# The first product of groups 3 to 6 of a routed attention and ELU kernel: four of seven block products cut once more into seven small ones

## The chip, the cores and the metric

The kernel runs on one core of a Trainium2 chip. Time is device time in microseconds (us) for one execution. The kernel before takes 914.18 us, the median of 3 runs (912.76 to 914.26). The profile comes from one further execution.

## What is computed

```python
attn = routing_attention(q, k, v, centroids)          # [4, 8, 768, 64], only within equal clusters
x = attn.transpose(0, 2, 1, 3).reshape(3072, 512)
h = x @ w_in                                          # [3072, 512] @ [512, 2048]: the first product
g = where(h > 0, h, exp(min(h, 0)) - 1)               # ELU
out = g @ w_out                                       # [3072, 2048] @ [2048, 512]: the second product
```

All matmuls spoken of here are float32. The weights arrive as float64 and are turned into float32 on the chip during the attention.

## The kernel before, in words

**Stages.** Until about 340 us the core computes the attention and leaves x transposed in `xT`. Then the 3072 tokens are worked off in six groups of 512 (`k_` = 0 to 5; the text counts them as groups 1 to 6). Each group has a first product with ELU, which fills `g`, and a second product.

**First product** (`unit`, line 765). The 2048 hidden columns are cut into fourths (`u` = 0 to 3). Within a fourth the product is a 2x2 block product done in seven block products for eight (Strassen in Winograd's form): M1 = a11·x11 and M5 = s1·t1, M6 = s2·t2, M2 = a12·x21, then s3·t3, s4·x22 and a22·t4. Here t1, t2, t3 and t4 are sums of blocks of x (`x_sum_step`, line 690, made on GpSimd for the next group by `next_group`, line 1027), and s2, s3, s4 are sums of blocks of w_in, which lie in DRAM and are loaded into `w_tmp` (`w_step`, line 709) once per fourth. One block product (`block_product`, line 736) is four float32 matmuls of 128x128 weights by 256 columns; the profile lists each matmul as two records, so a block product is "x8". The results are gathered in four PSUM banks b1 to b4 by copies on ScalarE (lines 779, 791, 799), adds on VectorE (lines 792, 801) and by letting TensorE add onto what a bank holds. ELU is `elu_exp` (exp on ScalarE, line 749, then a clamp on GpSimd, line 750) and `elu` (VectorE, line 753). What is late of a fourth is put into `behind` and issued by `flush_all` in the next.

**Second product** (`second_product`, line 1060). Its seven units M1 to M7 are each once more cut into seven small products for eight (m1 to m7). A small product (`small_product`, line 921) is four matmuls of 128x128 weights by 128 columns. The sums of blocks of w_out, with some blocks themselves, lie in DRAM as a table (`table_steps`, line 866) and stream through ten slots of 256 KB (`fetch`, line 915), each refilled as soon as the product that read it is done. For the left side VectorE makes t1 to t4 (`t_step`, line 959). The order on TensorE is written out by hand: m6, m2, m1 of the next unit, m7, m5 of the next unit, m3, m4. Where the last unit has no next one, two block products of the next group's first fourth (`ahead`) take those places.

**Order.** The schedule is written out by hand (`manual_schedule`): every engine, and SyncE's DMA queue (SP), executes its instructions in the order in which the Python code issues them, and an instruction that waits holds back what stands behind it on its engine. Group 1 has a plain second product (`second_product_plain`, line 1034, with eight block products per unit and no table).

Of the kernel before, what the change touches and what calls it, by code (L numbers as in the profile page):

```python
# [61 lines left out]
def main_path(ctx, tc, c, q, k, v, centroids, moe_w_in, moe_w_out, out):  # L62
# [85 lines left out]
    slots_w = [words_w[:, ts(n, 512)] for n in range(4)]  # L148
    slots_w += [sums_w[:, 1536 + 512 * n : 2048 + 512 * n] for n in range(5)]
    slots_w += [p_out[:, 4096:4608]]  # L150
    x_s = [x_sum[:, ts(n, GS)].rearrange("p (c n) -> p c n", n=QS) for n in range(3)]

    blocks = [(b, half, pr) for b in range(B) for half in range(2) for pr in range(NPR)]
# [550 lines left out]
        low, high = slice(QS * u, QS * u + QS), slice(DF // 2 + QS * u, DF // 2 + QS * u + QS)  # L704
        return w_in[:, :2, low], w_in[:, 2:, low], w_in[:, :2, high], w_in[:, 2:, high]

    w_far = [[far.tile([P, 512], F32, name=f"w_far{u}{n}") for n in range(3)] for u in range(4)]

    def w_step(k_, u, n):

        a11, a12, s1, a22 = w_parts(u)
        s2, s3, s4 = (w_tmp[:, m] for m in range(3))
        flat = spare[:, 0, ts(n, 512)]
        if k_ > 0:
            nc.sync.dma_start(flat, w_far[u][n])
            return
        if n == 0:
            nc.gpsimd.tensor_tensor(s2, s1, a11, op=Alu.subtract)
        elif n == 1:
            nc.gpsimd.tensor_tensor(s3, a22, s2, op=Alu.subtract)  # L720
        else:
            nc.gpsimd.tensor_tensor(s4, a12, s2, op=Alu.subtract)
        nc.gpsimd.dma_start(w_far[u][n], flat)

    def blanks(s):

# [9 lines left out]
    def block_product(bank, left, right, first):  # L736
        for f in range(2):
            for ch in range(2):
# [6 lines left out]
                    skip_group_check=True,  # L745
                )

    def elu_exp(to, bank):
        nc.scalar.activation(to, bank.rearrange("p (f n) -> p f n", f=2), Act.Exp)  # L749
        nc.gpsimd.tensor_scalar(to, to, 1.0, 0.0, op0=Alu.min, op1=Alu.max)  # L750

    def elu(to, bank):
        nc.vector.scalar_tensor_tensor(  # L753
            to, to, -1.0, bank.rearrange("p (f n) -> p f n", f=2), op0=Alu.add, op1=Alu.max
        )

    behind = []
# [136 lines left out]

    WHICH = {"m1": "q11", "m2": "q12", "m3": "s4", "m4": "q22", "m5": "s1", "m6": "s2", "m7": "s3"}
    HERE = {"m1": (0, 0), "m2": (0, 1), "m4": (1, 1), "m5": (1, 0)}
    order = [(0, "m1"), (0, "m5")]
    for n in range(len(UNITS)):
        nxt = n + 1 if n + 1 < len(UNITS) else None
        for m in ("m6", "m2", "m1+", "m7", "m5+", "m3", "m4"):  # L900
            if m[2:]:
                if nxt is not None:
                    order.append((nxt, m[:2]))
            else:
                order.append((n, m))
    streamed = [
        (a, WHICH[m])
        for _ in range(1, N // GS)
        for n, m in order
        for a in (UNITS[n][1],)  # L910
        if (a, WHICH[m]) in far_w
    ]
    fetched, used = 0, 0

    def fetch():
        nonlocal fetched
        if fetched < len(streamed):
            nc.sync.dma_start(slots_w[fetched % len(slots_w)], far_w[streamed[fetched]])
            fetched += 1

    def small_product(bank, left, right, first, last=True):
        for f in range(4):
# [9 lines left out]
    def banks_of(k_, n):  # L932
        return sets[(k_ + n) % 2]

    def part_product(k_, n, m):

        nonlocal used
        _, a, b = UNITS[n]
        b1, b2, b3, b4 = banks_of(k_, n)
        bank = {"m1": b1, "m5": b4, "m6": b2, "m2": b1, "m7": b3, "m3": b2, "m4": b3}[m]  # L940
        left = {
            "m1": lambda: part_g(b, 0, 0),
            "m2": lambda: part_g(b, 1, 0),
            "m3": lambda: part_g(b, 1, 1),
            "m4": lambda: t_of["t4"],
            "m5": lambda: t_of["t1"],
            "m6": lambda: t_of["t2"],
            "m7": lambda: t_of["t3"],
        }[m]()
        if (a, WHICH[m]) in far_w:  # L950
            assert streamed[used] == (a, WHICH[m])
            right = slots_w[used % len(slots_w)].rearrange("p (f m) -> p f m", m=P)
            used += 1
            small_product(bank, left, right, m in ("m1", "m5"))
            fetch()
        else:
            small_product(bank, left, part_w(a, *HERE[m]), m in ("m1", "m5"))

    def t_step(n, t):
        if n >= len(UNITS):  # L960
            return
        b = UNITS[n][2]
        q11, q12, q21, q22 = (part_g(b, i, j) for i in range(2) for j in range(2))
        to = t_of[t]
        if t == "t1":
            nc.vector.tensor_tensor(to, q12, q11, op=Alu.subtract)
        elif t == "t2":
            nc.vector.tensor_tensor(to, q22, t_of["t1"], op=Alu.subtract)
        elif t == "t3":
            nc.vector.tensor_tensor(to, q22, q12, op=Alu.subtract)  # L970
        else:
            nc.vector.tensor_tensor(to, q21, t_of["t2"], op=Alu.subtract)
# [54 lines left out]
    def next_group(k_):  # L1027
        if k_ + 1 < N // GS:
            for n in range(4):
                x_sum_step(k_ + 1, n)  # L1030
            for n in range(3):
                w_step(k_ + 1, 0, n)

    def second_product_plain(k_, early_on):

        for n in range(len(UNITS)):
            _, a, b = UNITS[n]
            for q_ in range(4):
                for j in range(2):
                    small_product(  # L1040
                        banks_of(k_, n)[q_],
                        part_g(b, j, q_ % 2),
                        part_w(a, q_ // 2, j),
                        j == 0,
                        j == 1,
                    )
                if n == 0 and q_ == 0:
                    flush_all()
                    early_on()
                elif n == 2 and q_ == 1:  # L1050
                    verdict()
                take(k_, n, q_)
            taken(k_, n)
            if n < 3:
                g_step(n, 0)
                g_step(n, 1)
            if n == 2:
                next_group(k_)

    def second_product(k_, ahead):  # L1060

        m5s = [stage[:, 2, ts(n, P)] for n in range(2)]
        u3s = [stage[:, 2, 256 + P * n : 384 + P * n] for n in range(2)]

        def first(n):
            part_product(k_, n, "m1")
            b1, b2 = banks_of(k_, n)[:2]
            nc.scalar.copy(b2[:, :P], b1[:, :P])

        def second(n):  # L1070
            part_product(k_, n, "m5")
            nc.scalar.copy(m5s[n % 2], banks_of(k_, n)[3][:, :P])

        first(0)
        flush_all()
        second(0)
        last = len(UNITS) - 1
        for n in range(len(UNITS)):
            b1, b2, b3, b4 = (x[:, :P] for x in banks_of(k_, n))
            part_product(k_, n, "m6")  # L1080
            nc.scalar.copy(b3, b2)
            if n > 0:
                take(k_, n - 1, 2)
                take(k_, n - 1, 3)
                taken(k_, n - 1)
            t_step(n + 1, "t1")
            nc.vector.tensor_tensor(b2, b2, m5s[n % 2], op=Alu.add)
            t_step(n + 1, "t2")
            part_product(k_, n, "m2")
            take(k_, n, 0)  # L1090
            if 1 <= n <= 3:
                g_step(n - 1, 0)
            if n < last:
                first(n + 1)
            else:
                next(ahead, None)
            part_product(k_, n, "m7")
            nc.scalar.copy(u3s[n % 2], b3)
            t_step(n + 1, "t3")
            nc.vector.tensor_tensor(b4, b4, u3s[n % 2], op=Alu.add)  # L1100
            if 1 <= n <= 3:
                g_step(n - 1, 1)
            if n < last:
                second(n + 1)
            else:
                next(ahead, None)
            if n == last and k_ + 1 == N // GS:
                take(k_, n, 3)
            part_product(k_, n, "m3")
            take(k_, n, 1)  # L1110
            if n == last and k_ + 1 == N // GS:
                store_tile(k_, 1, nc.scalar)
            part_product(k_, n, "m4")
            t_step(n + 1, "t4")
            if n == 1:
                next_group(k_)
        if k_ + 1 < N // GS:
            for q_ in (3, 2):
                take(k_, last, q_)
            taken(k_, last)  # L1120
        else:
            take(k_, last, 2)
            store_tile(k_, 0, nc.scalar)

    def findings():
        ok = c["ok"]
# [78 lines left out]
        next(table, None)  # L1205
        next(table, None)

    ahead = None
    for k_ in range(1, N // GS):
        for u in range(4):  # L1210
            if k_ == 1 and u < 2:
                blanks((k_ + u) % 2)
            fill = fill_table if k_ == 1 else None
            run(ahead if ahead is not None and u == 0 else unit(k_, u, fill=fill))
        ahead = unit(k_ + 1, 0) if k_ + 1 < N // GS else iter(())
        second_product(k_, ahead)


@with_exitstack
# [259 lines left out]
```

## Time and profile before

| | |
|---|---|
| median of 3 runs | 914.18 us |
| the profiled execution | 913.61 us |
| its span on the core | 911.7 us |
| TensorE busy | 900.3 us, 99% |
| VectorE busy | 674.0 us, 74% |
| ScalarE busy | 416.9 us, 46% |
| GpSimd busy | 201.7 us, 22% |
| granted TensorE clock | 0.998 |

The span is what the hardware profiler saw on the core; 1.91 us of the profiled execution lie around it. In the views, PE is TensorE's matmuls and PEld its weight loads, DVE is VectorE, ACT ScalarE, POOL GpSimd, SP SyncE. L739 is line 739 of the kernel. A line of the timeline gives start, duration, engine, line, operation, output<-input, shapes and count, and in square brackets the idle time before with what ended it. Matmul records overlap: the time of a product is read from one start to the next start, not from the duration.

### The profile page before, as it was taken

To read this page: it belongs to the slowest core of one execution; us is meant where nothing else is said; L and a number is where in the kernel's file an instruction comes from. 1 tells how busy PE (TensorE), PEld (TensorE's weight loads), DVE (VectorE), ACT (ScalarE), POOL (GpSimd) and SP (SyncE) were. 2 spreads that over 40 slices of the span, in tenths; PEclk is the share of its full clock that TensorE was granted. 3 is DMA by queue.
4 is the path that set the end of the run, shared out by engine and by line. 5 is a ranking of instruction groups with operands and counts; after the bars stand their busy time and mean duration, and the time that the engine had idled before them with its cause. 6 is when DMAs were issued, how large, how long until landed. Compare 5 with 4: busy or idle time off the path is not lost.

```text
span 911.7 us, 15852 instructions
## 1 busy us (share of the span) xinstructions
PE 900.3 (99%) x6086; PEld 685.3 (75%) x6089; DVE 674.0 (74%) x980; ACT 416.9 (46%) x819; POOL 201.7 (22%) x197
## 2 busy tenths in 40 slices
PE   9999999999999999999999999999999999999997
PEld 5444444444444448899988998999899989998997
DVE  4799999999999996982389843684369445953575
ACT  6767787777768764310133223322332233213321
POOL 1022122131304326750025002400131013102200
PEclk9999999999999999999999999999999999999999
DMA  7755554354325431110297852185218621762172
GB/s 211 184 108 158 133 136 116 96 113 120 67 86 140 146 109 65 48 45 2 90 316 263 285 168 69 42 278 178 70 36 272 191 59 46 252 207 62 38 224 90
DMA packets 143331, 121.22 MB, mean 133 GB/s; under 512 B 88208, under 2 KB 104592, under 8 KB 142224
## 3 DMA queue, kind: packets, MB, share of 16 engines
q1 hardware_dynamic: 141712, 115.41, 43.4%
q0 software_dynamic: 1248, 4.20, 1.5%
q8 instruction: 50, 0.82, 0.4%
q10 hardware_dynamic: 288, 0.52, 0.2%
q14 instruction: 33, 0.27, 0.1%
HBM read 100.96 MB, written 18.09 MB: 131 GB/s over the span
## 4 chain that ended last, share of the span: by engine, by line
PE 86%; DVE 9%; POOL 2%; issue 1%; DMA 1%; ACT 1%; SPq 0%; DVEq 0%; POOLq 0%; ACTq 0%
PE bank L923 23%; PE bank L739 22%; PE banks L495 11%; PE o_bank L533 11%; PE o_bank L739 4%; PE o_bank L923 4%; PE banks L508 3%; PE d_bank L923 2%; PE d_bank L551 2%; PE d_bank L739 2%; DVE sums_w L525 1%; PE d_bank L424 1%; DVE sums_w L520 1%; PE banks L574 1%; DVE sums_w L526 1%
## 5 line engine op out<-in xcount | busy, mean ns | idle before, releaser
L517 ACT ACTIVATE p_out<-banks 128x768 f32<-128x768 f32 x192 | 155.2, 812 | 26.8 <-PE banks L508 25.4
L750 POOL TENSOR_SCALAR kq_g<-kq_g 128x512 f32<-128x512 f32 x96 | 71.5, 753 | 389.9 <-ACT kq_g L749 389.8
L533 PE MATMUL o_bank<-p_out,kq_g 128*64 128x384 f32 x768 | 129.3, 486 | 0.0
L533 PEld LDWEIGHTS o_bank<-p_out,kq_g 128*64 128x64 f32 x768 | 55.1, 137 | 68.8 <-issue 63.1
L753 DVE SCALAR_TENSOR_TENSOR kq_g<-kq_g,bank 128x512 f32<-128x512 f32 x72 | 48.3, 684 | 67.0 <-POOL kq_g L750 67.0
L739 PE MATMUL bank<-xT,w_in 128*128 128x256 f32 x384 | 90.7, 379 | 0.1
L569 POOL TENSOR_TENSOR xT<-xT,sums_w 128x384 f32<-128x384 f32 x32 | 35.4, 1105 | 222.1 <-DVE sums_w L566 173.7
L739 PEld LDWEIGHTS bank<-xT,w_in 128*128 128x128 f32 x384 | 72.6, 190 | 10.1
L739 PE MATMUL bank<-x_sum,w_in 128*128 128x256 f32 x288 | 68.0, 379 | 0.0
L739 PE MATMUL bank<-xT,spare 128*128 128x256 f32 x288 | 66.3, 379 | 0.7 <-DVE bank L792 0.7
L923 PE MATMUL bank<-w_out,kq_g 128*128 128x128 f32 x512 | 62.9, 275 | 0.0
L520 DVE TENSOR_TENSOR sums_w<-p_out 128x1536 f32<-128x1536 f32 x32 | 57.1, 1785 | 7.6 <-ACT p_out L517 7.6
L525 DVE TENSOR_TENSOR sums_w<-sums_w,p_out 128x1536 f32<-128x1536 f32 x32 | 59.0, 1845 | 3.3 <-DVE sums_w L520 0.5
L739 PEld LDWEIGHTS bank<-xT,spare 128*128 128x128 f32 x288 | 54.6, 190 | 8.4 <-issue 1.0
L923 PEld LDWEIGHTS bank<-w_out,kq_g 128*128 128x128 f32 x512 | 60.4, 192 | 0.3
L739 PEld LDWEIGHTS bank<-x_sum,w_in 128*128 128x128 f32 x288 | 54.6, 190 | 7.3
L749 ACT ACTIVATE kq_g<-bank 128x512 f32<-128x512 f32 x72 | 42.0, 597 | 39.0 <-PE bank L739 37.4
L983 DVE TENSOR_TENSOR kq_g<-kq_g 128x1024 f32<-128x1024 f32 x36 | 45.0, 1258 | 2.7 <-PE bank L923 2.7
L460 POOL TENSOR_SCALAR kq_g<-w_out,big,minus 128x768 bf16<-128x768 bf16 x16 | 34.1, 2142 | 46.0 <-ACT w_out L453 46.0
L495 PE MATMUL banks<-x_sum,xT 64*128 64x384 f32 x192 | 39.8, 492 | 0.0
L495 PE MATMUL banks<-kq_g 64*128 64x384 f32 x192 | 39.6, 491 | 0.0
L495 PE MATMUL banks<-x_sum,kq_g 64*128 64x384 f32 x192 | 39.6, 491 | 0.0
(240 smaller groups left out, 1709.5 us busy)
## 6 DMA issues: line engine op xcount, KB each, us to landing
spare<-w_far SPq DMA_DIRECT2D x60, 256.0 KB, 2.7
kq_g<-in_v_dram SPq DMA_DIRECT2D x32, 384.0 KB, 3.6
sums_w<-far_s_s SPq DMA_DIRECT2D x40, 256.0 KB, 4.1
words_w<-far_s_s SPq DMA_DIRECT2D x29, 256.0 KB, 3.6
out_dram<-p_out SPq DMA_DIRECT2D x22, 256.0 KB, 2.5
w_out<-in_q_dram SPq DMA_DIRECT2D x112, 48.0 KB, 2.4
words_w<-far_a_s SPq DMA_DIRECT2D x21, 256.0 KB, 3.7
sums_w<-far_s_q SPq DMA_DIRECT2D x21, 256.0 KB, 3.2
```

The source lines that it names most:

```text
L495: nc.tensor.matmul(s[:, e, :HS], lhsT=kT[b % 2][pr][rows, ts(kt, P)], rhs=qT[half][pr][rows], start=True, stop=False,)
L517: nc.scalar.activation(probs[kt], s[:, :, :HS], Act.Exp, scale=SCALE)
L520: nc.vector.tensor_tensor(add_to, probs_all[:, : 4 * HS], probs_all[:, 4 * HS : 8 * HS], op=Alu.add)
L525: nc.vector.tensor_tensor(add_to, add_to, probs_all[:, 8 * HS :], op=Alu.add)
L533: nc.tensor.matmul(o_bank[64 * e : 64 * e + 64, :HS], lhsT=v_raw[n % 2][:, e, kt], rhs=probs[kt][:, e], start=(kt == 0), stop=(kt == NT - 1),)
L569: nc.gpsimd.tensor_tensor(x_of(n), x_of(n), r_of, op=Alu.mult)
L739: nc.tensor.matmul(bank[:, ts(f, QS)], lhsT=left[:, ch, ts(f, P)], rhs=right[:, ch], start=first and f == 0 and ch == 0, stop=ch == 1, ski ...
L749: nc.scalar.activation(to, bank.rearrange("p (f n) -> p f n", f=2), Act.Exp)
L750: nc.gpsimd.tensor_scalar(to, to, 1.0, 0.0, op0=Alu.min, op1=Alu.max)
L753: nc.vector.scalar_tensor_tensor(to, to, -1.0, bank.rearrange("p (f n) -> p f n", f=2), op0=Alu.add, op1=Alu.max)
L923: nc.tensor.matmul(bank[:, :P], lhsT=left[:, f], rhs=right[:, f], start=first and f == 0, stop=last and f == 3, skip_group_check=True,)
L983: nc.vector.tensor_tensor(b[to][:, f], b[x][:, f], b[y][:, f], op=op)
```

## The change

For groups 3 to 6 (`k_` = 2 to 5, `FIRST_IN = 2`) the first product is done in two parts.

Part one is a chain of four further units ("In units") behind the seven units of the *previous* group's second product, in one loop `chain` that takes the place of `second_product`. The units are M1, M6, M5, M2 of the first product, now over all 2048 hidden columns at once, and each is cut into seven small products m1 to m7. A small product here is four matmuls of 128x128 weights by 128 tokens, into one bank of 128x512. Their left sides stream from a new table in DRAM (`far_in`, 16 tiles of 256 KB), made on VectorE during the plain second product of group 1 (`in_table_steps`) and by three adds in place (`in_place`). The differences of x blocks (128x128) are made on GpSimd. The results go to the places of `g` (`InUnit.take`): after the last unit, c11 is finished up to its ELU, and c12, c21, c22 hold what the remaining three block products add to.

Part two (`rest_of_group`) goes by fourths: ScalarE copies c21 and c12 from `g` into banks (`begin_rest`), TensorE adds s3·t3, s4·x22 and a22·t4, then comes ELU. Its first step stands where the last In unit has no next unit.

The loads of s2 per fourth fall away (s2 lies in DRAM as one tensor `s2_far` that also serves the new table); s3 and s4 have new places in SBUF (`rest_places`). `next_group` of group 1 moves from unit 3 to unit 6 of the plain second product. Groups 1 and 2 keep `unit`, and the seven units of the second product keep their work.

```diff
+    def w_far_of(u, n):
+        if n == 0:
+            return s2_far[:, u // 2, :, ts(u % 2, QS)]
+        return w_far[u][n - 1].rearrange("p (c n) -> p c n", c=2)
...
+    IN_UNITS = [("M1", "a11"), ("M6", "s2"), ("M5", "s1"), ("M2", "a12")]
+    FIRST_IN = 2
...
+    def in_table_steps():
+        dead = [xT[:, ch, :GS] for ch in range(KC)]
+        held = [flat[:, ts(n, 512)] for n in range(6)]
...
+        for a, s1, (s3, s2, s4) in (
+            ("a11", dead[0], held[3:]), ("s1", dead[0], dead[1:]),
+            ("a12", held[0], held[3:]), ("s2", dead[2], held[:3]),
+        ):
+            if a == "s2":
+                keep_far()
+                for n in range(4):
+                    nc.sync.dma_start(dead[n], s2_far[:, n // 2, n % 2])
...
+            nc.vector.tensor_tensor(s3, q11, q21, op=Alu.subtract)
+            yield
+            nc.vector.tensor_tensor(s1, q21, q22, op=Alu.add)
+            keep_far()
+            yield
+            nc.vector.tensor_tensor(s2, s1, q11, op=Alu.subtract)
+            yield
+            nc.vector.tensor_tensor(s4, q12, s2, op=Alu.subtract)
...
+    class InUnit:
...
+        def product(self, m):
...
+            for f in range(4):
+                nc.tensor.matmul(bank[:, ts(f, P)], lhsT=left[:, ts(f, P)], rhs=right,
+                    start=m in ("m1", "m5") and f == 0, stop=True, skip_group_check=True)
+            done()
+        def t(self, t):
...
+            nc.gpsimd.tensor_tensor(xt[t], x, y, op=Alu.subtract)
+        def take(self, q_):
...
+            if self.n == 0:
+                nc.scalar.copy(c11, b)
+            elif self.n == 1:
+                nc.vector.tensor_tensor(c21, b, c11, op=Alu.add)
+            elif self.n == 2:
+                nc.vector.tensor_tensor(c12, b, c21, op=Alu.add)
+                nc.scalar.copy(c22, b)
+            else:
+                nc.vector.tensor_tensor(b, b, c11, op=Alu.add)
+                elu_exp(c11, bank)
+                behind.append(lambda: elu(c11, bank))
+        def note(self, at):
+            if at == "m4" and self.n == 2:
+                rest_load(1)
...
+    def seven_first(u):
+        u.product("m1")
+        nc.scalar.copy(u.banks[1], u.banks[0])
+    def seven_second(u):
+        u.product("m5")
+        nc.scalar.copy(u.m5, u.banks[3])
...
+    def chain(units, ahead):
...
+        for i, u in enumerate(units):
...
+            u.product("m6")
+            nc.scalar.copy(b3, b2)
+            if i > 0:
+                units[i - 1].take(2)
+                units[i - 1].take(3)
+                units[i - 1].taken()
+            if nxt:
+                nxt.t("t1")
+            nc.vector.tensor_tensor(b2, b2, u.m5, op=Alu.add)
+            if nxt:
+                nxt.t("t2")
+            u.product("m2")
+            u.take(0)
+            u.note("m2")
+            if nxt:
+                seven_first(nxt)
+            else:
+                next(ahead, None)
+            u.product("m7")
+            nc.scalar.copy(u.u3, b3)
...
+            nc.vector.tensor_tensor(b4, b4, u.u3, op=Alu.add)
+            u.note("m7")
+            if nxt:
+                seven_second(nxt)
...
+            u.product("m3")
+            u.take(1)
...
+            u.product("m4")
...
+        else:
+            u.take(3)
+            u.take(2)
+            u.taken()
+    REST = [(1, 2), (0, 3)]
+    def rest_places(u):
+        return [w_tmp[:, n] if n < 3 else o_rest for n in REST[u % 2]]
+    def rest_load(u):
+        for n, place in enumerate(rest_places(u)):
+            nc.sync.dma_start(place, w_far_of(u, n + 1))
+    def rest_of_group(k_):
...
+        for u in range(4):
+            _, b2, b3, b4 = sets[(k_ + u) % 2]
...
+            def begin_rest(v):
...
+                nc.scalar.copy(as_part(n3, c21), g[:, hi, :QS])
+                nc.scalar.copy(as_part(n2, c12), g[:, lo, QS:])
+            if u == 0:
+                begin_rest(0)
+            block_product(b3, s3, t3, False)
+            nc.vector.tensor_tensor(as_part(b4, c22), as_part(b3, c22), c22, op=Alu.add)
+            flush_all()
+            if u == 0:
+                yield
+            block_product(b2, s4, x22, False)
+            if u < 2:
+                rest_load(u + 2)
+            elu_exp(c22, b4)
+            if u < 3:
+                flush_all()
+                begin_rest(u + 1)
+            t_step(0, f"t{u + 1}")
+            elu_exp(c12, b2)
+            elu(c22, b4)
+            block_product(b3, a22, t4, False)
+            def rest(c12=c12, c21=c21, c22=c22, b2=b2, b3=b3):
+                elu_exp(c21, b3)
+                elu(c12, b2)
+                nc.vector.tensor_tensor(c12, c22, c12, op=Alu.subtract)
+                elu(c21, b3)
+            behind.append(rest)
...
     def second_product_plain(k_, early_on):
+        in_table = in_table_steps()
...
                 take(k_, n, q_)
+                if q_ < 3 and n > 0:
+                    next(in_table, None)
...
-            if n == 2:
+            if n == 5:
+                run(in_table)
                 next_group(k_)
...
     for k_ in range(1, N // GS):
-        for u in range(4):
-            if k_ == 1 and u < 2:
-                blanks((k_ + u) % 2)
-            fill = fill_table if k_ == 1 else None
-            run(ahead if ahead is not None and u == 0 else unit(k_, u, fill=fill))
-        ahead = unit(k_ + 1, 0) if k_ + 1 < N // GS else iter(())
-        second_product(k_, ahead)
+        if k_ < FIRST_IN:
+            for u in range(4):
+                if u < 2:
+                    blanks((k_ + u) % 2)
+                run(unit(k_, u, fill=fill_table))
+        else:
+            run(rest)
+        rest = rest_of_group(k_ + 1) if k_ + 1 < N // GS else iter(())
+        chain(units_behind(k_), rest)
```

## The prediction

> **What bounds the kernel now.** I read the page first, then a table by stage, then TensorE's timeline at a group's ends, then the other engines' timelines there. The page's busy times and its chain of waits:
>
> ```profile
> PE 900.3 (99%) x6086; PEld 685.3 (75%) x6089; DVE 674.0 (74%) x980; ACT 416.9 (46%) x819; POOL 201.7 (22%) x197
> ...
> PE 86%; DVE 9%; POOL 2%; issue 1%; DMA 1%; ACT 1%; SPq 0%; DVEq 0%; POOLq 0%; ACTq 0%
> ```
>
> TensorE sets the time. Is it so in the groups that change? The table by stage, for one whole period of group 3 to 4 (start of a second product to start of the next):
>
> ```profile
> 585.28:677.40 92.12, 92.12 (x617) 86.33 (x616) 55.43 (x99) 27.92 (x72) 16.50 (x21) 1.00 0.45 140
> ```
>
> Columns: length, then busy time of PE, PEld, DVE, ACT, POOL, the granted clock, the DMA share and GB/s. TensorE is busy for all 92.12 us at clock 1.00. So any time in which TensorE newly waits is paid in full. TensorE's timeline gives the prices of its products, start to start:
>
> ```profile
> 435.98 7.31 PE L923 MATMUL bank<-w_out,kq_g 128*128 128x128 f32 x64
> 443.12 0.38 PE L728 MATMUL o_bank<-blank 128*128 128x512 bf16 x1
> 443.34 0.38 PE L728 MATMUL bank<-blank 128*128 128x512 bf16 x1
> 443.56 1.89 PE L739 MATMUL bank<-xT,w_in 128*128 128x256 f32 x8
> ...
> 453.92 1.89 PE L739 MATMUL bank<-x_sum,w_in 128*128 128x256 f32 x8
> ```
>
> Eight small products take 443.12-435.98 = 7.14 us, 0.893 each. Six block products take 453.92-443.56 = 10.36 us, 1.727 each. Check: 49 x 0.893 + 28 x 1.727 = 43.8+48.3 = 92.1 us, the period. There is no slack in it.
>
> **TensorE's work.** One of M1, M6, M5, M2 costs four block products now, 4 x 1.727 = 6.91 us for all fourths; in seven small ones 7 x 0.893 = 6.25. Over four such products a group gains 2.62 us: 77 x 0.893 + 12 x 1.727 = 89.5 for 92.1. Four groups: 10.5 us, the most that there is to win. The small products read and write other tiles, but the row has the same shape, and such rows hold 0.893 whatever tile they read.
>
> **Hand-over rows.** What new waits come is worked out from these lines of the timeline:
>
> ```profile
> 634.24 1.89 PE L739 MATMUL bank<-xT,w_in 128*128 128x256 f32 x8
> 634.49 0.57 ACT L791 COPY bank<-o_bank 128x512 f32<-128x512 f32 x1 [2.98 <-PE o_bank L739]
> 635.09 0.70 DVE L792 TENSOR_TENSOR o_bank<-o_bank,spare 128x512 f32<-128x512 f32 x1 [2.10 <-ACT bank L791]
> ...
> 636.16 0.60 ACT L749 ACTIVATE kq_g<-bank 128x512 f32<-128x512 f32 x1 [1.10 <-PE bank L739]
> 636.85 0.61 POOL L750 TENSOR_SCALAR kq_g<-kq_g 128x512 f32<-128x512 f32 x1 [42.58 <-ACT kq_g L749]
> 637.49 0.69 DVE L753 SCALAR_TENSOR_TENSOR kq_g<-kq_g,bank 128x512 f32<-128x512 f32 x1 [1.70 <-POOL kq_g L750]
> ```
>
> A product that ends as the next starts (634.24) has its reader going at 634.49: 0.25. ScalarE's end 635.06 to VectorE 635.09 is 0.03, 636.76 to 636.85 on GpSimd 0.09; I take 0.06 for each. Behind one another on one engine, 512 columns cost less than alone:
>
> ```profile
> 392.54 0.60 ACT L749 ACTIVATE kq_g<-d_bank 128x512 f32<-128x512 f32 x1 [0.69 <-DVE d_bank L801]
> 393.04 0.59 ACT L749 ACTIVATE kq_g<-bank 128x512 f32<-128x512 f32 x1
> ```
>
> So 0.50 on ScalarE; VectorE's rows at 585.53 and 586.13 give 0.60-0.61. After a stop TensorE loses some 0.08 more (the product at 498.42, after a wait of 0.56, takes 0.99 instead of 0.893).
>
> **The In units** put 512 columns where second-product units have 128. Per unit of 6.25 us ScalarE has four copies and at most four takes, 8 x 0.59 = 4.7 us; VectorE two adds and at most four takes, 6 x 0.70 = 4.2. Within a unit TensorE leaves two products, 1.79 us, between m6 and m7 for the copy b2 to b3, and as much between m7 and m4; the copy needs 0.25+0.57+0.06 = 0.88. Cost nothing, with 0.9 us spare; if another wait of that size got ahead of the copies, it would show in every unit. GpSimd's 128x128 subtractions have no row; they lie between nothing and the 1.27 us of the 128x512 one (L695). I take 0.4, and they have 1.8 us or more, so either end costs nothing.
>
> **Wait 1, into the fourths.** The last In unit (M2) has no next one, so behind its m2 TensorE meets s3·t3 of the first fourth, which adds onto a bank that `begin_rest` must fill. That copy stands on ScalarE behind exp of `take(0)`, exp behind VectorE's add of c11, the add behind b2 += m5, that behind the copy b2 to b3, that behind m6. From m6's end: copy 0.25 to 0.83; b2 += m5 from 0.88, the next VectorE op 0.61 later at 1.49, the add ends at 2.18; exp at 2.24, the next ScalarE op 0.50 later at 2.74; the copy from SBUF to a bank (no row; from 0.25, L1068's 128 columns, to 0.60, L749; I take 0.585, L799) ends at 3.32, TensorE goes at 3.38. It was ready after m2, at 0.89. **2.49 us**. Queued behind the waiting product are m7, m3, m4 and all that follows, and nothing else is there for TensorE to do. Bounds with 0.25 for the copy and 0.03 hand-overs: 2.1; with 0.60 steps on ScalarE and 0.1 hand-overs: 2.9.
>
> **Wait 2, second fourth.** Its bank b3 is the last unit's, read by the ELU of c11. From m4's end: VectorE adds for q3 (0.26) and q2 (0.87 to 1.56); exp, behind q3's, 1.62 to 2.22; clamp 2.28 to 2.89; ELU 2.95 to 3.64; ScalarE's copy 3.70 to 4.28; TensorE 4.34. Meanwhile it has s4·x22 and a22·t4, 3.45. **0.89 us** (bounds 0.5 and 1.4).
>
> **Waits 3 and 4, third and fourth fourths.** Their b3 is read until the ELU of c21 of two fourths ago. From the end of s3·t3: b4 = b3 + c22 at 0.26, then on VectorE ELU of c12, the subtraction, ELU of c21, three steps of 0.61 later at 2.09 to 2.78; copy 2.84 to 3.42; TensorE 3.48, against 3.45: 0.03. But the subtraction reads two SBUF tensors and falls beside GpSimd's clamp of c22 (1.68 to 2.29). Such rows stretch beside GpSimd:
>
> ```profile
> 586.84 0.69 DVE L818 TENSOR_TENSOR kq_g<-kq_g 128x512 f32<-128x512 f32 x1
> ...
> 398.55 1.03 DVE L818 TENSOR_TENSOR kq_g<-kq_g 128x512 f32<-128x512 f32 x1
> ```
>
> Alone 0.69, beside a busy GpSimd 1.03. With half to three quarters of the overlap I take +0.25: **0.28 us each** (bounds 0 and 0.6). After the last fourth nothing new is late: the second product's m1 reads c11, long done, and its bank b1 is free.
>
> **Sum of a group:** 2.49+0.89+2 x 0.28 = 3.94, with 4 x 0.08 for restarts 4.26, less 2.62: **+1.64 us**. Four groups: +6.6. Bounds: 2.1+0.5+0+0.2 = 2.8, that is +0.2 a group; 2.9+1.4+1.2+0.4 = 5.9, +3.3 a group.
>
> The clock row above shows 1.00, and no wait of TensorE behind the attention is longer than 0.66 us, so nothing here shows what a stop of 2.5 us does to it. The Trainium skill ("TensorE: Matmul & The Clock Gate", "HAM oscillation") warns of idle gaps over about 3.4 us, after which TensorE runs at half speed until it has again been busy for so long. By that rule 2.5 us is short of the limit, and the sum stays; if the gate closed all the same, an estimate from that page is 1.7 us lost per stop, 7 us in all.
>
> **Streams.** Per group 16 new table loads on SP, four w_far loads fewer. In the chain 16 of 28 small products stream, thinner than the 21 in a row of s4, s3 and s2 before, which ran without a wait on 2.7 to 4.4 us landings and ten slots (8.9 us ahead). The table by stage has the DMA share at 0.24 in the fourths of this period (631.6 to 677.4), 0.66 in the second product. SP's new loads of s3, s4 stand behind the product that frees their place, with 7 us until they are read. Cost 0; if the stream fell behind, up to 1 us a group.
>
> **One-time parts.** Sixteen VectorE steps in group 1's plain product, 16 x 0.69 = 11.0 us, 17 if stretched, lie in 28 idle us of VectorE (22.1 busy of 50.2), two units ahead of any bank reuse. `next_group` moves behind them; GpSimd's sums keep their place, since nothing precedes them on its queue, but SP's three `w_tmp` loads now wait for the last table writes. Those are ready some 3 us behind unit 6 (436), so written at 442 and the loads at 445 to 446; s2 is read at 447.0. Between 0 and 3 us once; I take 0.3. The three adds in place in the chain of group 2 (37.4 busy of 47.7 on VectorE) and the s2 writes in rows of 1 KB in group 1: between -0.3 and 1 together, taken as nothing.
>
> **Total:** +6.6+0.3 = +6.9. The profiled execution, 911.7 of span and 1.9 around it, would go from 913.6 to 920.5. It lies 0.6 under the median 914.2; on the median I forecast **921.1 us**.
>
> **Rivals.**
> *Balance.* Waits 2 to 4 shrink to their lower bounds and wait 1 is near its own: 2.2+0.5+0+0.2 = 2.9, +0.3 a group: 915.4. For it: 0.03 us is all that decides waits 3 and 4. Against: wait 2 has five hand-overs and no spare.
> *Faster.* ScalarE's copy doesn't end behind exp: were c21 in its bank in time, wait 1 would be nothing, and 0.89+0.56+0.24-2.62 = -0.9 a group gives 910.5; with waits 2 to 4 gone as well 903.7. Place: the hand-over in the last In unit. It decides where all waits of a group stay under 2.62. For it: c21 is ready long before. Against: the code issues the copy behind exp, and ScalarE's rows follow the code's order everywhere.
> *Much slower.* VectorE stretched throughout the fourths, its t-steps too (0.69 becomes 1.55 beside GpSimd's two-input sums): upper bounds, +3.3 a group, a late stream 1 us more, one-time 3 us: 914.2+17+3 = 934.
>
> **Chances.** Forecast case (over 916 to 928) 0.70, much slower 0.06, balance within 0.2% 0.13, faster 0.11. About 0.2% (1.8 us) is what a measurement of this kernel can tell from no change. Slower is 0.76, same 0.13, faster 0.11. The bounds of the four groups give 915 to 928; I reach down to 914.5 into the balance case and up to 928.
>
> **What would show it.** TensorE's timeline should have one stop of 2.5 us per chain before the first fourth's s3·t3, ended by ScalarE's copy in `begin_rest`, one of 0.9 before the second fourth's, and two small ones; four periods of 93.8 instead of 92.1 us; small products at 0.893 throughout the In units, with no stop. The forecast is wrong if that copy is no releaser, if stops in a period sum to less than 2.6, or if the In units themselves stop.

## The result and the profile after

The changed kernel takes 922.72 us (median of 4 runs, 921.68 to 924.64), the kernel before 914.22 (median of 4): slower, ratio 1.0099, 95% interval 1.0078 to 1.0119. The forecast was 921.1. The profiled execution is 922.16 us, its span 919.9.

First the page's busy times and its chain of waits, as shown of before:

```profile
PE 896.4 (97%) x6473; PEld 689.1 (75%) x6473; DVE 726.1 (79%) x1063; ACT 450.7 (49%) x883; POOL 242.6 (26%) x261
...
PE 84%; DVE 9%; ACT 2%; POOL 2%; issue 2%; DMA 0%; SPq 0%; DVEq 0%; ACTq 0%; POOLq 0%
```

TensorE is busy 3.9 us less, in a span 8.2 us longer, and ScalarE has 2% of the chain of waits, for 1% before. The table by stage, for the second and the fourth period of a chain (start of one second product to start of the next):

```profile
586.57:681.90 95.33, 92.25 (x714) 88.14 (x713) 65.17 (x115) 36.43 (x88) 26.49 (x36) 0.98 0.56 169
776.91:870.27 93.36, 90.57 (x714) 86.93 (x713) 65.53 (x115) 36.42 (x88) 26.71 (x36) 1.00 0.57 172
```

Before, every column of busy TensorE time equalled the length. Now 2.8 to 3.1 us of a period stand empty, and the second period has a granted clock under 1. The four periods take 94.18, 95.33, 95.01 and 93.36 us, where before had 92.94, 92.12, 92.10 and 92.1: 1.24, 3.21, 2.91 and 1.26 more.

TensorE's timeline at the end of the first chain shows where the empty time is:

```profile
557.53 1.06 PE L1064 MATMUL o_bank<-spare,sums_w 128*128 128x128 f32 x8
558.42 1.06 PE L1064 MATMUL bank<-xT,w_in 128*128 128x128 f32 x8
561.75 1.99 PE L748 MATMUL bank<-xT,spare 128*128 128x256 f32 x8 [2.27 <-ACT bank L1219]
563.58 1.05 PE L1064 MATMUL bank<-spare,sums_w 128*128 128x128 f32 x8
...
570.51 1.99 PE L748 MATMUL bank<-xT,spare 128*128 128x256 f32 x8 [0.52 <-ACT bank L1219]
```

L1064 is a small product of an In unit (0.89 us from start to start, as priced), L748 a block product, L1219 the copy of c21 in `begin_rest`. The last In unit's m2 starts at 558.42 and gives TensorE free at 559.31; s3·t3 of the first fourth starts at 561.75, 2.44 us later. Behind it, 0.10 more goes on the restart. ScalarE's and VectorE's timelines in that stop are the chain that the prediction wrote down:

```profile
558.67 0.57 ACT L1151 COPY bank<-o_bank 128x512 f32<-128x512 f32 x1 [0.53 <-PE o_bank L1064]
559.16 1.08 ACT L1094 COPY kq_g<-bank 128x512 f32<-128x512 f32 x2
560.61 0.60 ACT L761 ACTIVATE kq_g<-bank 128x512 f32<-128x512 f32 x1 [0.37 <-DVE bank L1096]
561.10 0.59 ACT L1219 COPY bank<-kq_g 128x512 f32<-128x512 f32 x1
```

VectorE's steps between them:

```profile
559.28 0.70 DVE L1158 TENSOR_TENSOR o_bank<-o_bank,p_out 128x512 f32<-128x512 f32 x1 [0.26 <-ACT bank L1151]
559.88 0.69 DVE L1096 TENSOR_TENSOR bank<-bank,kq_g 128x512 f32<-128x512 f32 x1
```

Copy b2 to b3 (L1151), b2 += m5 (L1158), the add of c11 (L1096), exp (L761), and only then the copy of c21 (L1219), which needs nothing of all that.

In the second and third chain something more happens. TensorE's timeline there:

```profile
655.40 3.39 PE L748 MATMUL bank<-xT,spare 128*128 128x256 f32 x8 [2.56 <-ACT bank L1219]
658.58 1.38 PE L1064 MATMUL bank<-spare,sums_w 128*128 128x128 f32 x8
659.80 1.06 PE L1064 MATMUL bank<-xT,sums_w 128*128 128x128 f32 x8
...
750.44 2.86 PE L748 MATMUL bank<-xT,spare 128*128 128x256 f32 x8 [2.27 <-ACT bank L1219]
753.09 1.89 PE L1064 MATMUL bank<-spare,sums_w 128*128 128x128 f32 x8
```

The table by stage around the four stops, cut where the granted clock changes (the first column behind the length is busy TensorE time; the last three are granted clock, DMA share, GB/s):

```profile
560.27:563.68 3.41, 1.93 (x9) 1.73 (x10) 0.30 (x1) 1.60 (x3) 0.61 (x1) 1.00 0.26 96
652.43:655.84 3.41, 0.85 (x6) 0.63 (x5) 1.30 (x2) 3.04 (x6) 0.61 (x1) 1.00 0.64 221
655.84:659.25 3.41, 3.41 (x12) 2.76 (x11) 0.36 (x1) 0.01 (x1) 0.00 (x0) 0.50 0.00 0
748.00:751.41 3.41, 1.14 (x7) 0.87 (x6) 1.26 (x2) 2.52 (x5) 0.61 (x1) 1.00 0.61 188
751.41:754.83 3.42, 3.42 (x14) 3.04 (x13) 1.28 (x2) 0.00 (x0) 0.00 (x0) 0.50 0.00 0
843.57:846.99 3.42, 1.54 (x7) 1.39 (x8) 0.71 (x2) 1.97 (x4) 0.61 (x1) 1.00 0.37 132
```

The granted clock is 0.50 for 3.41 us behind the stops of the second and the third chain, and the two falls begin 95.57 us apart, 28 times 3.413. In the 3.41 us ahead of a fall TensorE was idle for 2.56 and 2.27 us. Carried on in steps of 3.413 us, the same grid cuts the stops of the first and the fourth chain in two: their most idle steps (the first and the last line) have 1.48 and 1.88 us, and no fall follows.

What do the falls cost? s3·t3 takes 3.18 us (655.40 to 658.58) instead of 1.83, and m7 1.22 instead of 0.89: 1.68 us lost; in the third chain 0.82 + 0.82 + 0.02 = 1.66. So the two periods have 1.25 us from the waits, 1.7 from the clock, and the second one 0.3 more from a stop of 2.73: ScalarE's copy b2 to b3 starts that much later there. Why it does stays open; the same chain has it in the experiment with the shorter stop (1.77 for 1.48).

### The profile page after: what moved, and what is told of

It reads as the page before. It is cut to its first block, busy times and chain, and to the rows that moved or that the text cites. A ratio compares the mean times of both kernels' runs of the same rounds, so it can differ in the third digit from the quotient of the medians.

```text
span 919.9 us, 17057 instructions
## 1 busy us (share of the span) xinstructions
PE 896.4 (97%) x6473; PEld 689.1 (75%) x6473; DVE 726.1 (79%) x1063; ACT 450.7 (49%) x883; POOL 242.6 (26%) x261
## 4 chain that ended last, share of the span: by engine, by line
PE 84%; DVE 9%; ACT 2%; POOL 2%; issue 2%; DMA 0%; SPq 0%; DVEq 0%; ACTq 0%; POOLq 0%
PE bank L994 22%; PE bank L748 12%; PE banks L498 12%; PE o_bank L536 11%; PE bank L1064 8%; PE o_bank L994 4%; PE banks L511 3%; PE d_bank L554 2%; PE o_bank L748 2%; PE d_bank L994 2%; PE o_bank L1064 1%; DVE kq_g L765 1%; PE d_bank L427 1%; DVE sums_w L528 1%; PE d_bank L1064 1%
## 5 line engine op out<-in xcount | busy, mean ns | idle before, releaser
L762 POOL TENSOR_SCALAR kq_g<-kq_g 128x512 f32<-128x512 f32 x96 | 74.8, 791 | 169.3 <-ACT kq_g L761 169.2
L748 PE MATMUL bank<-xT,spare 128*128 128x256 f32 x256 | 63.7, 396 | 12.1 <-ACT bank L1219 11.5
L748 PEld LDWEIGHTS bank<-xT,spare 128*128 128x128 f32 x256 | 48.2, 194 | 23.7 <-ACT bank L1219 16.6
L748 PE MATMUL bank<-x_sum,w_in 128*128 128x256 f32 x224 | 52.9, 379 | 0.0
L761 ACT ACTIVATE kq_g<-bank 128x512 f32<-128x512 f32 x68 | 39.4, 595 | 26.0 <-PE bank L748 11.5
L765 DVE SCALAR_TENSOR_TENSOR kq_g<-kq_g,bank 128x512 f32<-128x512 f32 x68 | 45.4, 680 | 7.8 <-POOL kq_g L762 6.2
L748 PEld LDWEIGHTS bank<-x_sum,w_in 128*128 128x128 f32 x224 | 42.6, 190 | 5.8
L1082 POOL TENSOR_TENSOR spare<-x_sum 128x128 f32<-128x128 f32 x16 | 7.3, 455 | 142.3 <-PE bank L1064 80.4
L498 PE MATMUL banks<-kq_g,xT 64*128 64x384 f32 x192 | 39.6, 491 | 0.0
```

What stands on the lines that cost most here:

```text
L498: nc.tensor.matmul(s[:, e, :HS], lhsT=kT[b % 2][pr][rows, ts(kt, P)], rhs=qT[half][pr][rows], start=True, stop=False,)
L748: nc.tensor.matmul(bank[:, ts(f, QS)], lhsT=left[:, ch, ts(f, P)], rhs=right[:, ch], start=first and f == 0 and ch == 0, stop=ch == 1, ski ...
L761: nc.scalar.activation(to, as_part(bank, to), Act.Exp)
L765: nc.vector.scalar_tensor_tensor(to, to, -1.0, as_part(bank, to), op0=Alu.add, op1=Alu.max)
```

## The experiments

Theory A: the added time is the stop at the hand-over with three smaller waits, and the falls of the clock follow from the stop. Theory B: the clock falls for another reason. Theory C: the In units' own work costs the time. The kernel before, run beside them, took 913.58 us (first four), 913.83 (next two) and 913.76 (last).

**The stop taken out.**

```diff
             if nxt:
                 seven_first(nxt)
-            else:
-                next(ahead, None)
             u.product("m7")
             nc.scalar.copy(u.u3, b3)
+            if not nxt:
+                next(ahead, None)
...
             if u == 0:
                 begin_rest(0)
+                yield
             block_product(b3, s3, t3, False)
...
             flush_all()
-            if u == 0:
-                yield
```

> Edit: only the hand-over in the last In unit. The two copies of begin_rest stand behind the copy of u3, and s3*t3 of the first fourth stands behind m4 instead of between m2 and m7. The same products, copies and adds are done. Theory A (the time comes from the stop at the hand-over, and the two falls of the clock follow from the stop): the stop of 2.44 us and its restart go, four times, 10.2 us; the clock stays at 1.00 through all chains, 3.3 us more; wait 2 stays at 0.6 to 0.7. 922.7 - 13.5 = 909.2 us (907.5 to 911). Theory B (the falls of the clock have nothing to do with the stop): the stop goes, but falls to 0.5 remain in two of four chains, 912.5 us. Theory C (the small products or the 512-column work around them cost the time, and TensorE waits elsewhere when this stop is gone): 916 to 922 us, with new stops inside the In units.

Measured: 911.2 us (910.48 to 911.76), 11.5 less than the changed kernel, and faster than before: 0.9971, interval 0.9960 to 0.9983. The granted clock is 1.00 through all four chains. The time is 2 us more than expected. TensorE's timeline of this kernel has no stop before s3·t3, but a new one before m4 of the last In unit, in all four chains (the second line is wait 2, which stays):

```profile
561.94 1.13 PE L1064 MATMUL bank<-spare,w_in 128*128 128x128 f32 x8 [0.46 <-ACT p_out L1167]
...
568.66 1.99 PE L748 MATMUL bank<-xT,spare 128*128 128x256 f32 x8 [0.41 <-ACT bank L1219]
```

m4 waits 0.63 us for the copy of u3 (L1167), as ScalarE's timeline shows:

```profile
560.72 0.60 ACT L761 ACTIVATE kq_g<-bank 128x512 f32<-128x512 f32 x1 [0.37 <-DVE bank L1096]
561.22 0.58 ACT L1167 COPY p_out<-bank 128x512 f32<-128x512 f32 x1
```

The same exp, still waiting for VectorE, now holds the copy of u3. C is out: it expected 916 us or more, and apart from this m4, in the hand-over itself, no product of an In unit stops.

**The stop made longer.**

```diff
             if u == 0:
+                for _ in range(2):
+                    nc.scalar.copy(as_part(b3, c21), c21)
                 begin_rest(0)
```

> Edit: the first copy of begin_rest is done three times over instead of once, in the last In unit only (the same values to the same bank), so that ScalarE is about 1.0 us later and the stop is 3.4 us instead of 2.44. Theory A: 4 x 1.0 = 4 us more, and with the longer stop the clock falls to 0.5 in more of the four chains, up to all, 1.65 us each: 922.7 + 4 + 3.3 = 930 us (927 to 931). Theory B: 4 us more and clock falls that are as many as before: 926.7.

Measured: 931.3 us (930.72 to 932.63). The stop is 3.68 us (559.43 to 563.11 in the first chain), and the product behind it is slow in all four chains:

```profile
563.11 3.43 PE L748 MATMUL bank<-xT,spare 128*128 128x256 f32 x8 [3.51 <-ACT bank L1219]
...
659.14 3.78 PE L748 MATMUL bank<-xT,spare 128*128 128x256 f32 x8 [3.51 <-ACT bank L1219]
...
756.35 2.98 PE L748 MATMUL bank<-xT,spare 128*128 128x256 f32 x8 [3.51 <-ACT bank L1219]
...
852.61 3.65 PE L748 MATMUL bank<-xT,spare 128*128 128x256 f32 x8 [3.51 <-ACT bank L1219]
```

Four falls for two; B expected as many as before. They begin at 562.64, 658.21, 757.20 and 852.77, which is 28, 29 and 28 times 3.413 us apart, each behind 3.41 us in which TensorE was idle for 2.56 us or more. The second lasts two such steps:

```profile
658.21:665.04 6.83, 5.89 (x19) 5.18 (x20) 1.28 (x2) 1.74 (x4) 0.00 (x0) 0.50 0.00 0
```

This longer fall, and a stop that grew by 1.24 us instead of 1.0, put the time just above the 927 to 931 expected.

**The stop made shorter.**

```diff
+            if not nxt:
+                next(ahead, None)
             u.take(0)
             u.note("m2")
...
             if u == 0:
                 begin_rest(0)
+                yield
```

> Edit: the two copies of begin_rest are issued ahead of take(0) of the last In unit, so that they no longer stand behind exp; s3*t3 stays between m2 and m7. The copy now follows the two c22 copies of the unit before, ready at about 2.3 us after the end of m6, so the stop is 1.5 us instead of 2.44. Theory A: 4 x 0.95 = 3.8 us less and no fall of the clock, 3.3 less: 915.6 us (914 to 917.5). Theory B: 3.8 us less, falls remain: 918.9. If the stop does not shrink, exp was not what held the copy: 922.7.

Measured: 915.46 us (914.55 to 916.24). The copy did stand behind exp. Stops are 1.48 us (1.77 in the second chain), and the product behind them has its normal 1.99 in all four; no fall of the clock:

```profile
561.04 1.99 PE L748 MATMUL bank<-xT,spare 128*128 128x256 f32 x8 [1.31 <-ACT bank L1221]
...
653.73 1.99 PE L748 MATMUL bank<-xT,spare 128*128 128x256 f32 x8 [1.60 <-ACT bank L1221]
```

**The stop filled.** Five matmuls are added whose result nothing uses.

```diff
                 begin_rest(0)
+                for _ in range(5):
+                    nc.tensor.matmul(sets[k_ % 2][0][:, :QS], lhsT=a22[:, 0, :P], rhs=x22[:, 0],
+                        start=True, stop=True, skip_group_check=True)
             block_product(b3, s3, t3, False)
```

> Edit: five float32 matmuls of 256 columns, 5 x 0.43 = 2.2 us, are put on TensorE ahead of s3*t3 of the first fourth, into a bank that nobody reads before it is begun anew; everything else is as in the changed kernel. They fit into the stop of 2.44 us. Theory A (the clock falls because TensorE stands still): s3*t3 starts when it did, the clock stays at 1.00, and only the 3.3 us of the clock come back: 919.4 us (918.5 to 920.5). Theory B: falls of the clock remain, 922.7 us. If the matmuls were on the path beyond the stop: more than 922.7.

Measured: 919.58 us (918.74 to 920.60). The timeline of the first chain:

```profile
558.86 2.32 PE L1225 MATMUL bank<-xT,w_in 128*128 128x256 f32 x10
561.29 1.99 PE L748 MATMUL bank<-xT,spare 128*128 128x256 f32 x8
```

s3·t3 still starts 2.44 us after TensorE was free for it (558.85), so the wait itself is all there; only the idleness is gone, and with it the falls: around each of the four stops TensorE is idle for at most 0.6 us in 10 to 15 us, and the clock is 1.00. That is 3.1 us less than the changed kernel with every wait in its place. It settles A against B.

**The copy of u3 ahead of exp,** on top of the first experiment:

```diff
             u.product("m2")
-            u.take(0)
-            u.note("m2")
+            if nxt or ending:
+                u.take(0)
+                u.note("m2")
             if nxt:
                 seven_first(nxt)
             u.product("m7")
             nc.scalar.copy(u.u3, b3)
-            if not nxt:
+            if not nxt and not ending:
+                u.take(0)
+                u.note("m2")
                 next(ahead, None)
```

> Edit: on top of e1_stop_gone, in the last In unit take(0) with its exp is issued behind m7 and the copy of u3, instead of ahead of m7. In e1_stop_gone the profile shows a new stop of 0.63 us before m4, because the copy of u3 stands on ScalarE behind an exp that waits for VectorE. Theory A: this stop and its restart go, 4 x 0.73 = 2.9 us less than e1_stop_gone (911.2): 908.3 us, against a kernel before at 913.6. Wait 2 (0.57 us) and waits 3 and 4 (0.2 with the restart) stay. If the copy of u3 is not what m4 waits for: 911.2.

Measured: 909.08 us (908.24 to 909.60), ratio to before 0.9945, interval 0.9928 to 0.9962. The stop before m4 is gone from the timeline; of the stops in the changed groups the list of TensorE's waits has wait 2 alone (waits 3 and 4 are too short for it).

**The order of the ELU steps,** on top of that:

```diff
             block_product(b3, s3, t3, False)
+            if u == 0:
+                behind.pop(0)()
+                behind[1], behind[2] = behind[2], behind[1]
...
                 elu_exp(c21, b3)
+                elu(c21, b3)
                 elu(c12, b2)
                 nc.vector.tensor_tensor(c12, c22, c12, op=Alu.subtract)
-                elu(c21, b3)
```

> Edit: on top of e5_u3_first, the order of the ELU steps on VectorE: in the first fourth the ELU of c11's first quarter goes ahead of b4 = b3 + c22 and those of the quarters whose banks b2 and b3 are wanted next come before the last; in all fourths the ELU of c21 goes ahead of that of c12 and of the subtraction. Theory A (the four waits are all that stands between the changed kernel and the 10.5 us of fewer columns): wait 2 falls to 0.1 or less and waits 3 and 4 go with their restarts, 4 x (0.57 + 0.1 + 0.4) = 4.3 us less than e5_u3_first: 904.0 us, 9.6 under the kernel before (913.6). If TensorE stops elsewhere once these are gone, the sum of a period over 89.5 us shows by how much: 905 to 908.

Measured: 912.13 us (911.21 to 914.11), 3 us *more* where 5 less, or 1 to 4 less, was expected. The waits of the fourths are gone, but TensorE's timeline shows a new one in three of the four second products that follow:

```profile
590.61 1.16 PE L994 MATMUL d_bank<-w_out,p_out 128*128 128x128 f32 x8 [1.89 <-DVE p_out L1259]
```

VectorE's timeline ahead of the first of them:

```profile
585.78 0.69 DVE L765 SCALAR_TENSOR_TENSOR kq_g<-kq_g,bank 128x512 f32<-128x512 f32 x1 [1.55 <-POOL kq_g L762]
586.39 0.68 DVE L765 SCALAR_TENSOR_TENSOR kq_g<-kq_g,o_bank 128x512 f32<-128x512 f32 x1
587.10 1.78 DVE L1250 TENSOR_TENSOR kq_g<-kq_g 128x512 f32<-128x512 f32 x1
588.81 1.75 DVE L1259 TENSOR_TENSOR p_out<-kq_g 128x512 f32<-128x512 f32 x1
```

VectorE stands 1.55 us for a clamp (L762) with two ready steps queued behind it. Then its subtraction and t1 fall beside GpSimd's sums of x and take 1.8 us instead of 0.69. In the three earlier fourths the same order is right, because the clamp is done by then. The three stops are 2.06 us each, and no fall of the clock follows any of them.

**The old order in the last fourth only:**

```diff
                 elu_exp(c21, b3)
-                elu(c21, b3)
+                if u < 3:
+                    elu(c21, b3)
                 elu(c12, b2)
                 nc.vector.tensor_tensor(c12, c22, c12, op=Alu.subtract)
+                if u == 3:
+                    elu(c21, b3)
```

> Edit: e6_all_waits, but the ELU of c21 goes first on VectorE only in the first three fourths; in the last fourth the order is again ELU of c12, subtraction, ELU of c21. The profile of e6_all_waits (912.1) shows the waits in the fourths gone and a new stop of 1.9 us in the next second product, three times, ended by VectorE's t1 of its second unit: in the last fourth VectorE waits 1.55 us for GpSimd's clamp of c21 and only then does the ELU of c12, the subtraction and t1, the latter two stretched to 1.8 us beside GpSimd's sums of x. Theory A: with the old order there this stop goes (e5_u3_first has none), 3 x 2.0 = 6.0 us: 906 us, between 904 and 907.5, some 7.5 under the kernel before. If the stop comes from GpSimd's sums alone, whatever the order on VectorE: 912.

Measured: 904.18 us (903.86 to 905.18), ratio to before 0.9897, interval 0.9880 to 0.9913: 9.6 us under before and 18.5 under the change as it was. The table by stage for its second period, to be held against 92.12 of before:

```profile
583.36:673.29 89.93, 89.93 (x715) 87.32 (x714) 65.22 (x115) 36.66 (x88) 25.75 (x36) 1.00 0.55 179
```

TensorE is busy throughout again, and from start to start (583.36 to 673.17) the period is 89.81 us, 0.3 above the 89.5 of its products. That is 2.3 us a group. The step from 912.13 to 904.18 is 2 us more than expected. In the two profiles the difference is 6.9 us (spans 909.0 and 902.1), of which the three stops with their restarts are 3 x 2.16 = 6.5; the rest of the medians' difference was not followed up.

## Why the prediction was right

| term of a group, us | forecast | measured in the profile |
|---|---|---|
| fewer columns on TensorE | -2.62 | -2.62 (0.89 a small product, 1.73 a block product) |
| wait 1, into the fourths | 2.49 | 2.44 (2.73 once) |
| wait 2 | 0.89 | 0.69 (569.82 to 570.51) |
| waits 3 and 4, with restarts | 0.36 each | 0.20 each |
| restarts of waits 1 and 2 | 0.16 | 0.20 |
| m4 of the last In unit | 0 | 0.11 |
| sum | +1.64 | +1.2; periods +1.24 and +1.26 where the clock held |
| fall of the clock | 0 | 1.7, in two of four chains |
| one-time parts | 0.3 | 0.05 (chain of group 2 starts at 492.39 for 492.34) |

*What bounds the kernel* held: TensorE had no slack, and the four new waits were paid in full.

*The mechanism* was the forecast one, with its releaser: ScalarE's in-order queue put the copy of c21 behind an exp that waits for VectorE. Moving the copy shortened the stop by 0.96 us; moving TensorE's product away removed it. The rival "faster", whose place was this hand-over, named its condition rightly: once all waits of a group stay under 2.62 us, the same products make the kernel faster (909.08 and 904.18).

*Sizes that were off.* Waits 2 to 4 were put too high by 0.2 us each with restarts. For waits 3 and 4 the stretch of the subtraction was the wrong row: in the fourths VectorE's subtraction took 0.69 (L1244 at 669.25), while the clamp on GpSimd beside it took 1.07 instead of 0.61. The subtraction had started first, and it was the clamp that grew. Of the 0.2 us, 0.1 is the restart.

*The clock* was the step that failed, and it hid the error above. The prediction took the falls at nothing, because the Trainium skill's page "TensorE: Matmul & The Clock Gate" ("HAM oscillation") puts the limit at idle gaps over about 3.4 us, and said "By that rule 2.5 us is short of the limit, and the sum stays", with 1.7 us a stop, 7 in all, if the gate closed anyway. The price was right, 1.66 and 1.68; the limit was not: stops of 2.44 and 2.73 us were enough in two of four cases. The measurement decides: 0 falls of 4 at 1.5 to 1.8 us, 0 of 3 at 2.06, 2 of 4 at 2.4 to 2.7, 4 of 4 at 3.7, none where the stop was filled. The same page ("What's actually happening") calls the window in which activity is watched free-running, 3413 ns. The traces agree: in both profiles with falls in the chains, these begin whole multiples of 3.413 us apart and last one or two such steps. That is why equal stops fell on both sides. What counted was not the length of the stop but TensorE's idle time within one step: in the profiles of all nine kernels, before and the experiments included, 2.27 us and more brought the half clock each time, 1.88 and less never did. Between the two no run here has a case. Where a stop lies on the grid is chance as far as the kernel goes: the four executions of the change had mean granted clocks of 0.996, 0.994, 0.993 and 0.996, so the number of falls was not always two.

So +1.25 x 4 = 5.0 from the waits, some 3.3 from the clock and 0.3 from the one longer stop make the 8.5 that was measured, where the forecast had 6.6 from the waits and 0.3 once. That the total came within 1.6 us is luck in part, two errors of opposite sign; with the stop filled, and so without the falls, the kernel takes 919.58 us, inside the range as well.

*Streams and In units* cost nothing, as forecast: no product of an In unit other than m4 of the last waits for anything, and no stop of TensorE behind the attention ends with a DMA.

## What to carry to other kernels

When TensorE is full, look at each place where one stage hands over to the next and write down what stands ahead of the first needed copy on its engine: an operand that is long ready is still late if its copy is issued behind an instruction that waits. Price such a stop twice, once for its length and once for the half clock behind it, which here cost 1.7 us behind two of four stops of 2.4 to 2.7 us and nothing behind stops up to 2.06. An order that helps in three fourths can hurt in the fourth one, where the value that it waits for comes later: check a reordering at every place where it applies.

## What the runs showed of the hardware that was not expected

- The granted clock fell to 0.50 after stops of TensorE as short as 2.44 us, though not after each; after 2.06 us and less never. The falls lie on a grid of 3.413 us, and what told them apart was the idle time in one step of it: 2.27 us or more against 1.88 or less. Five float32 matmuls in the stop kept the clock at 1.00.
- Beside each other, two-input rows of VectorE in SBUF and rows of GpSimd slowed down unequally, and in the rows looked at it was the one that started second that grew. A clamp that started 0.10 us behind VectorE's subtraction took 1.07 us for 0.61, the subtraction its 0.69. A subtraction that started 0.04 us behind one of GpSimd's sums (L700 at 587.06, 1.27 us, in the sixth experiment) took 1.78 for 0.69, and ended 0.55 behind it.
- GpSimd's 128x128 subtraction, which had no row before, takes 0.46 us in the In units (L1082), and ScalarE's copy from SBUF into a bank 0.59 (L1219), as fast as one from a bank.
